# The seven-product stage of a three-part kernel: sums of weights on GpSimd, roundings a step behind, blocks of 256 and 320 tokens

## Chip, cores and metric

One NeuronCore of a Trainium2 chip. The metric is the device time of one execution in microseconds (us). Engines are named as the profile names them: PE (TensorE matmul), PEld (its weight loads), DVE (VectorE), ACT (ScalarE), POOL (GpSimd), SP (SyncE, which issues most of the transfers).

## What is computed

```python
def reference(q, k, v, w_in, w_out, w_gate, w1, w2):
    # 1. attention: pairs of queries are averaged, 2 batches x 8 heads, 1152 keys, 576 queries, 64 wide
    q_pool = q.reshape(2, 8, 576, 2, 64).mean(axis=3)
    a = softmax(q_pool @ k.transpose(0, 1, 3, 2) / 8) @ v
    x = a.transpose(0, 2, 1, 3).reshape(1152, 512)
    # 2. dense layer, 512 -> 2048 -> 512; w_in and w_out are float64
    h = x @ w_in
    x = (h * tanh(softplus(h))) @ w_out
    # 3. eight experts, 512 -> 1024 -> 512, weighted by a gate with 8 Sinkhorn rounds
    P = sinkhorn(exp(x @ w_gate))
    return sum(P[:, e:e+1] * (relu(x @ w1[e]) @ w2[e]) for e in range(8))
```

All of it is float32 arithmetic. The change lies in part 2.

## The kernel before

**Precision.** Every matmul operand is split into a rounded high part and a remainder (`split_hi`, L81 on ACT, `split_lo`, L88 on DVE or POOL). A product of two split operands is three matmuls: low times high, high times low, high times high.

**Part 2, plain stage.** The 2048 columns of `w_in` are done in four groups `i` of 512. Group 0 goes by plain products: twelve banks of 128 columns by 384 tokens, `mish_step(k)` for k = 0 to 11 (12 matmuls each, L259), with one more step, k = 12, behind them. What a step puts on ACT: the Mish of the bank before it and the rounding of its result (L285, L81), copies of finished output blocks (`out_sum`, L874 on ACT for the first half of the columns, L876 on DVE for the second), then what `run` finds due on the lists `queue[...]` ("pool", "act", "dve", "dma"), each with a due step. Output blocks (`out_bank`, L867, six matmuls of 384 tokens) use three PSUM banks "o". From the step in which they are ready, at most two follow the bank's products. Sixteen come in the steps 3, 4 and 7 to 12, the last eight behind step 12.

**Weights.** A quarter of a group's float64 weights (128 x 512) comes by one transfer from SP (L154) into a raw tile. ACT scales both halves (L167, L169), DVE shifts and joins bits (L182, L187), and POOL adds the low part (`join`, L193). `load_w` gives each of these a due step. The raw tiles are taken in turn: `raw_tile` uses one of `raw_tags` tags, three during attention and two from step 3 on, because the third tag (`raw2`) then holds `ut`, the temporaries of the seven-product stage. For `w_in` of groups 1 to 3 the result stays in float32 in `w32`. For `w_out` it is rounded on ACT and its remainder is taken on POOL (L88).

**Part 2, seven-product stage.** Groups 1 to 3 replace the 2 x 2 block product (two halves of the columns' pairs, two batches of tokens, two halves of the depth) by seven products of sums. The input sums T1 to T4 are made once, during the plain steps (`X_WORK`: `whole_x` L907 and `less` L910 on DVE over 128 x 1152 elements, `t_hi` on ACT, `t_lo` on POOL or DVE). The sums of the weights are made for each group and each half `f` by `operands(i, f)`, seven steps: four sums (L945, DVE, 128 x 256), seven roundings (L81, ACT) and seven remainders (L88, POOL), into the tiles `slots0` (f = 0) or `slots1` (f = 1). `unit(i, f, j)` runs the seven products (L979, six matmuls each) for half f and token block j of 288, with the output sums on DVE (L984, through `t1`, `u2`, `u3` in `ut`), a copy on ACT (L1000), and Mish and rounding (L992, L81) one or two events later.

**Order.** `phase` writes the order out by hand: a string of "m" (a product) and "q" (an output block, `out_block`, 12 matmuls of 288 tokens, L1035, added on DVE at L1038). After each of them `run_all` issues what is due on the lists, and after each "m" one step of `operands` follows. Group 1 starts with the last eight plain output blocks between its products; groups 2 and 3 run four phases of seven products and four output blocks:

```python
EVEN = "mmmqmqmqmmq"
phase(unit(i, 0, 0), qs[:4], prep, EVEN)   # prep: operands(i, 1)
phase(unit(i, 1, 0), qs[4:], [], EVEN)
phase(unit(i, 0, 1), qs[:4], [], EVEN)
phase(unit(i, 1, 1), qs[4:], [] if last else operands(i + 1, 0), EVEN)
```

In `unit` the product order is 1, 6, 5, 2, 7, 3, 4. Product 2 is added to the bank of product 1 after the copy t1 has been taken; product 4 is added to the bank of 6 and 7 after `u3` has been formed from it. The engines take their instructions in the order of the program. `operands(1, 0)` starts at step k = NB - 2 = 10 (`raise_slots`, `first_ops`); its tile takes the place of the plain stage's weights.

Part 3 (gate, experts) follows and isn't touched.

Of the kernel before, what the change touches and what calls it, by code (L numbers as in the profile page):

```python
# [8 lines left out]
F32 = mybir.dt.float32  # L9
# [14 lines left out]
def pool_attention_mish_sinkhorn_kernel(  # L24
# [301 lines left out]
    with ExitStack() as actx:  # L326
# [322 lines left out]
        def run_av(n):  # L649
# [13 lines left out]
        load_w(0, 1, [(t, t + 1, t + 2, 0, 0) for t in evenly(T0 + 4, 1.25)], 1)  # L663
        load_w(1, 1, [tuple(T0 + x for x in t) for t in (
            (9, 10, 11, 12, 12.4), (10, 11, 12, 12.5, 13), (12.3, 13, 13.7, 14.3, 14.9), (13.6, 14.3, 15, 15.6, 16.2))], 0.7)
# [173 lines left out]
    raw_tags = 2  # L839
    ut = wraw.tile([P, 2 * GF], F32, tag="raw2", name="ut")  # L840
# [37 lines left out]
    HB = SQ // 2  # L878

    def tokens(b, j):  # L880
        return slice(b * SQ + j * HB, b * SQ + (j + 1) * HB)

# [32 lines left out]
    def t_lo(n, k, eng):  # L915
# [4 lines left out]
        3: [lambda: whole_x(0, "12"), lambda: whole_x(1, "11")],  # L920
        4: [lambda: less(1, 0, 1), lambda: t_hi("T1", 1), lambda: whole_x(2, "22")],
        5: [lambda: t_lo("T1", 1, o_), lambda: less(0, 2, 0), lambda: t_hi("T3", 0)],
        6: [lambda: less(1, 2, 1), lambda: t_hi("T2", 1), lambda: t_lo("T3", 0, o_)],
        7: [lambda: whole_x(2, "21"), lambda: t_lo("T2", 1, v_)],
        8: [lambda: less(2, 2, 1)],
        11: [lambda: t_hi("T4", 2)],
        12: [lambda: t_lo("T4", 2, v_)],
# [12 lines left out]
    def operands(i, f):  # L940

        w = w32(i)
        a = lambda r, d: w[:, 2 * d:2 * d + 2, (2 * f + r) * P:(2 * f + r + 1) * P]
        def add(out, x, y, op, eng=nc.vector):
            eng.tensor_tensor(out=out, in0=x, in1=y, op=op)  # L945

        def split(n, x):
            hi, lo = slot(f, n)
            split_hi(nc.scalar, hi, x)
            split_lo(nc.gpsimd, lo, x, hi)  # L950

        return [
            lambda: (split(1, a(0, 0)), add(s1, a(1, 0), a(1, 1), ALU.add)),
            lambda: (split(5, s1), add(a(1, 0), a(0, 0), a(1, 0), ALU.subtract)),
            lambda: (add(a(0, 0), s1, a(0, 0), ALU.subtract), split(6, a(0, 0))),
            lambda: (split(2, a(0, 1)), split(7, a(1, 0))),
            lambda: add(a(0, 1), a(0, 1), a(0, 0), ALU.subtract),
            lambda: split(3, a(0, 1)),
            lambda: split(4, a(1, 1)),
        ]  # L960

    t1, u2, u3 = (ut[:, n * HB:(n + 1) * HB] for n in range(3))

    def unit(i, f, j):

        box = {}

        def mult(n):
            xn, bn = PRODUCT[n]
            if n in OPENS:  # L970
                box[bn] = ps_h.tile([P, 512], F32, tag="h", name=f"m{i}{f}{j}{bn}")[:, 0:HB]
            wh, wl = slot(f, n)
            x_h, x_l = XT[xn] if xn[0] == "T" else XB[xn]
            js = slice(j * HB, (j + 1) * HB)
            ops = []
            for d in range(2):
                ops += [(wl[:, d], x_h[:, d, js]), (wh[:, d], x_l[:, d, js]), (wh[:, d], x_h[:, d, js])]
            for m, (a_, b_) in enumerate(ops):
                nc.tensor.matmul(  # L979
                    box[bn], lhsT=a_, rhs=b_, start=n in OPENS and m == 0, stop=n in SHUTS and m == len(ops) - 1,  # L980
                    skip_group_check=True)
# [43 lines left out]
    def out_block(i, b, j, dc):  # L1025
        ps = ps_o.tile([P, 512], F32, tag="o", name=f"po{i}{b}{j}{dc}")
        tl = tokens(b, j)
        ds_ = slice(dc * P, (dc + 1) * P)
        ops = []
        whi, wlo = w2t[i]  # L1030
        for cc in range(NFC):
            gh, gl = hidden(cc, tl.start, tl.stop)
            ops += [(wlo[:, cc, ds_], gh), (whi[:, cc, ds_], gl), (whi[:, cc, ds_], gh)]
        for n, (a, b_) in enumerate(ops):
            nc.tensor.matmul(ps[:, 0:HB], lhsT=a, rhs=b_, start=(n == 0), stop=(n == len(ops) - 1))  # L1035
        step_pend()
        o = acc[:, dc, tl]
        pend.append((0, lambda: nc.vector.tensor_tensor(out=o, in0=ps[:, 0:HB], in1=o, op=ALU.add)))  # L1038

# [17 lines left out]
    first_ops = []  # L1057
    for k in range(EARLY, NB + 1):
# [3 lines left out]
        if k == NB - 2:  # L1062
            raise_slots()
        if k >= NB - 2:
            for _ in range((2, 3, 2)[k - NB + 2]):
                first_ops.pop(0)()
# [7 lines left out]
    xctx.close()  # L1074
    spacer(mctx, 64, "spb", side="right")
    wb = mctx.enter_context(tc.tile_pool(name="wb", bufs=1, side="right"))
    slots[1] = tuple(wb.tile([P, 7, 2, P], F32R, name=f"slots1{x}") for x in "hl")
# [8 lines left out]
    def phase(ms, qs, prep, order, dt=DTQ):  # L1086
        ms, qs = list(ms), list(qs)
        for c in order:
            if c == "m":
                event(ms.pop(0), DTM)  # L1090
                if prep:
                    prep.pop(0)()
            else:
                event(qs.pop(0), dt)
        assert not ms and not qs and not prep

    EVEN = "mmmqmqmqmmq"
    qs = [lambda x=x: old_block(*x[2:]) for x in todo]
    for i in range(1, NG1):
        last = i == NG1 - 1  # L1100
        prep = operands(i, 1)
        if i == 1:
            phase(unit(i, 0, 0), qs, prep, "qqmqmqmqmqmqmmq", DTO)
            phase(unit(i, 1, 0), [], [], "mmmmmmm")
# [510 lines left out]
```

## Time and profile before

| what | us |
|---|---|
| median of 3 runs | 1235.11 (1234.12 to 1237.66) |
| the profiled execution | 1235.38 |
| its span, first to last instruction | 1233.5 |
| busy: PE / DVE / ACT / POOL | 1193.0 / 925.2 / 610.5 / 675.7 |

The difference between the profiled time and the span (1.9 us) lies outside the instructions. Busy time is summed over an engine's instructions; matmuls overlap, so a busy PE need not be a PE at its peak. "Idle before" names what ended an engine's wait.

### The profile page before, as it was taken

What the parts mean: (1) busy time and instruction counts of PE and PEld (TensorE: products, weight loads), DVE (VectorE), ACT (ScalarE), POOL (GpSimd) and SP (SyncE); (2) the same over time, 40 slices, a digit from 0 to 9 for tenths busy, and PEclk for the clock granted to TensorE, in tenths of its full rate; (3) what the DMA queues carried; (4) which work ended last, traced back from release to release, by engine and by line L of the source; (5) the groups of instructions that cost most, each with busy time, mean ns of one, the idle gap of its engine ahead of it and who ended that gap; (6) DMA issues with size and microseconds to landing.
All of it is one profiled execution on the core that took longest, in us unless ns stands there. A gap on an engine that the chain in (4) does not pass through costs nothing.

```text
span 1233.5 us, 23493 instructions
## 1 busy us (share of the span) xinstructions
PE 1193.0 (97%) x8775; PEld 1172.9 (95%) x8775; DVE 925.2 (75%) x1708; ACT 610.5 (49%) x1431; POOL 675.7 (55%) x777
## 2 busy tenths in 40 slices
PE   8999999997798999999999999999999999999998
PEld 7999999996788989999999999999999999999998
DVE  7899999976586765578876766866877767866865
ACT  7899999864465544352333333333233333333331
POOL 7567777324546344355865555555556654555552
PEclk9999999998899999999999999999999999999999
DMA  5788887632122211001111111011111111110112
GB/s 195 262 287 279 279 280 261 228 119 86 44 94 85 84 38 60 18 10 52 44 52 52 52 53 52 26 46 42 52 52 44 52 52 52 52 45 30 45 46 78
DMA packets 53122, 116.66 MB, mean 95 GB/s; under 512 B 7976, under 2 KB 23536, under 8 KB 53008
## 3 DMA queue, kind: packets, MB, share of 16 engines
q1 hardware_dynamic: 50560, 106.31, 26.1%
q0 software_dynamic: 2448, 8.85, 2.5%
q8 instruction: 70, 1.15, 0.4%
q14 instruction: 44, 0.36, 0.1%
HBM read 66.86 MB, written 2.40 MB: 56 GB/s over the span
## 4 chain that ended last, share of the span: by engine, by line
PE 83%; DVE 7%; ACT 3%; issue 2%; DMA 2%; POOL 1%; DVEq 0%; POOLq 0%; ACTq 0%
PE po L1517 30%; PE c L1352 25%; PE psS L513 6%; PE psA L614 5%; PE po L1035 4%; PE psT L593 3%; PE ph L259 3%; DVE e L518 1%; DVE etl L599 1%; DMA er<-e 1%; DMA raw<-in_moe_w_in_dram 1%; PE psk L448 1%; PE po L867 1%; DVE xf L907 1%; ACT raw L167 1%
## 5 line engine op out<-in xcount | busy, mean ns | idle before, releaser
L1517 PE MATMUL po<-wdbl,hhall 128*128 128x256 f32 x1080 | 298.7, 277 | 0.0
L1517 PE MATMUL po<-wdbh,hlall 128*128 128x256 f32 x1080 | 298.3, 276 | 0.0
L1517 PE MATMUL po<-wdbh,hhall 128*128 128x256 f32 x1080 | 298.3, 276 | 0.0
L88 POOL TENSOR_TENSOR wslotsl<-s,wslotsh 128x256 fp32r<-128x256 f32 x180 | 132.6, 746 | 226.9 <-ACT wslotsh L81 225.5
L1526 DVE SCALAR_TENSOR_TENSOR oacc<-po,Pm,oacc 128x512 f32<-128x512 f32 (+1 forms) x217 | 161.2, 747 | 90.0 <-PE po L1517 85.1
L1517 PEld LDWEIGHTS po<-wdbl,hhall 128*128 128x128 f32 x1080 | 202.8, 188 | 0.0
L1517 PEld LDWEIGHTS po<-wdbh,hlall 128*128 128x128 f32 x1080 | 202.7, 188 | 0.0
L1517 PEld LDWEIGHTS po<-wdbh,hhall 128*128 128x128 f32 x1080 | 202.7, 188 | 0.0
L1369 ACT ACTIVATE t<-c 128x384 f32<-128x384 f32 x80 | 39.1, 489 | 234.2 <-PE c L1352 234.2
L1389 ACT ACTIVATE hhall<-c 128x384 fp32r<-128x384 f32 x180 | 88.5, 492 | 127.7 <-DVE c L1385 125.1
L88 POOL TENSOR_TENSOR wslotsl<-rawu,wslotsh 128x256 fp32r<-128x256 f32 x120 | 90.6, 769 | 49.5 <-ACT wslotsh L81 49.5
L599 DVE TENSOR_TENSOR etl<-psT,eth 128x384 fp32r<-128x384 f32 (+1 forms) x240 | 108.3, 510 | 7.5 <-ACT eth L596 6.9
L518 DVE TENSOR_SCALAR_CACHE_REDUCE e<-psS 128x1152 f32<-128x1152 f32 x72 | 97.7, 1356 | 16.3 <-PE psS L513 12.5
L1390 DVE SCALAR_TENSOR_TENSOR hlall<-c,hhall 128x384 fp32r<-128x384 f32 x180 | 98.8, 549 | 2.1
L596 ACT ACTIVATE eth<-psT 128x384 fp32r<-128x384 f32 (+1 forms) x240 | 92.1, 472 | 6.3 <-PE psT L593 5.9
L1352 PE MATMUL c<-x2h,wslotsl 128*128 128x384 f32 x280 | 94.3, 337 | 0.0
L1352 PE MATMUL c<-x2l,wslotsh 128*128 128x384 f32 x280 | 94.1, 336 | 0.0
L1352 PE MATMUL c<-x2h,wslotsh 128*128 128x384 f32 x280 | 94.1, 336 | 0.0
L532 ACT ACTIVATE e<-e,nm 128x1152 f32<-128x1152 f32 x70 | 89.2, 1274 | 2.8 <-DVE e L518 1.8
L81 ACT ACTIVATE wslotsh<-s 128x256 fp32r<-128x256 f32 x180 | 72.1, 411 | 25.3 <-DVE s L1318 23.9
L513 PE MATMUL psS<-kT,qT 128*128 128x384 f32 x384 | 81.3, 347 | 1.7 <-DVE e L518 1.2
L614 PE MATMUL psA<-etl,vst 128*128 128x256 f32 (+1 forms) x288 | 80.9, 303 | 0.8 <-DVE rs L541 0.4
(776 smaller groups left out, 3315.1 us busy)
## 6 DMA issues: line engine op xcount, KB each, us to landing
er<-e SPq DMA_DIRECT2D x70, 576.0 KB, 4.2
rawd<-in_moe_w_dram SPq DMA_DIRECT2D x60, 256.0 KB, 2.8
rawu<-in_moe_w_dram SPq DMA_DIRECT2D x30, 384.0 KB, 3.0
raw<-in_moe_w_in_dram SPq DMA_DIRECT2D x16, 512.0 KB, 6.1
raw<-in_moe_w_out_dram SPq DMA_DIRECT2D x16, 512.0 KB, 3.4
vraw<-in_v_dram POOLq DMA_DIRECT2D x15, 288.0 KB, 4.5
kraw<-in_k_dram POOLq DMA_DIRECT2D x13, 288.0 KB, 4.3
qT<-qT SPq DMA_DIRECT2D x28, 128.0 KB, 3.5
```

The costliest lines, as they stand in the source:

```text
L88: eng.tensor_tensor(out=lo, in0=src, in1=hi.bitcast(F32), op=ALU.subtract)
L513: nc.tensor.matmul(ps[:, kb, 0:TH], lhsT=a, rhs=kt[:, kb * TH:(kb + 1) * TH], start=(n == 0), stop=(n == len(ops) - 1))
L518: nc.vector.tensor_scalar(sc, ps[:, :, 0:TH], -1.0, None, op0=ALU.mult, op1=ALU.min, accum_out=nm)
L532: nc.scalar.activation(e, sc, AF.Exp, bias=nm, scale=-1.0, accum_out=rsS[p][:, t:t + 1])
L596: nc.scalar.activation(eh[:, cs, o:o + b - a], ps[:, 0:3, a:b], AF.Copy)
L599: nc.vector.tensor_tensor(out=el[:, cs, o:o + b - a], in0=ps[:, 0:3, a:b], in1=eh[:, cs, o:o + b - a].bitcast(F32), op=ALU.subtract)
L614: nc.tensor.matmul(box["ps"][:, 0:n], lhsT=vst[p, j][:, c].rearrange("p a d -> p (a d)"), rhs=(el, eh)[which][:, c, 0:n], start=(c == 0 an ...
L1352: nc.tensor.matmul(cb[c], lhsT=a_, rhs=b_, start=FIRST[n] and m == 0, stop=LAST[n] and m == len(ops) - 1, skip_group_check=True)
L1389: nc.scalar.activation(hi, b, AF.Relu)
L1390: los.append(lambda: nc.vector.scalar_tensor_tensor(out=lo, in0=b, scalar=0.0, in1=hi.bitcast(F32), op0=ALU.max, op1=ALU.subtract))
L1517: nc.tensor.matmul(ps[:, c0:c0 + 256], lhsT=a, rhs=b[:, cs.start + c0:cs.start + c0 + 256], start=(n == 0), stop=(n == len(ops) - 1))
L1526: nc.vector.scalar_tensor_tensor(out=oa, in0=ps[:, 0:w], scalar=gate, in1=oa, op0=ALU.mult, op1=ALU.add)
```

## The change

The sums of `w_in`'s blocks (four per `operands`) go from DVE to POOL, and `operands` has eight steps in place of seven, in which the remainder of an operand is issued one step after its rounding. In `phase` a step of it follows each event, not only each product. `operands(1, 0)` starts at step 12, not 10: four steps there and four behind the next four output blocks. Group 1's phases are reordered. The work on T1 to T4 is spread over more steps, each rounding a step behind its sum, and the remainders of T2 and T4 go from DVE to POOL. The third raw tag stays in use until step 7, and the due steps of group 1's weights shift a little. The token blocks are 256 and 320 in place of twice 288.

```diff
@@ -660,9 +660,9 @@
         load_w(1, 0, [(t, t + 1, t + 2, T0 + j, T0 + j + 1) for j, t in enumerate(QUIET[4:])], 2, "dve", busy=True)
         load_w(1, 0, [None, None] + [(t, t + 1, t + 2, t + 3, t + 4) for t in (T0 + 1, T0 + 3)], 1, "dve")
         G1, GT = T0 + NB, 28 * DTM + 16 * DTQ
-        load_w(0, 1, [(t, t + 1, t + 2, 0, 0) for t in evenly(T0 + 4, 1.25)], 1)
+        load_w(0, 1, [(T0 + t, T0 + t + 1, T0 + t + 2, 0, 0) for t in (4, 5, 6, 7)], 1)
         load_w(1, 1, [tuple(T0 + x for x in t) for t in (
-            (9, 10, 11, 12, 12.4), (10, 11, 12, 12.5, 13), (12.3, 13, 13.7, 14.3, 14.9), (13.6, 14.3, 15, 15.6, 16.2))], 0.7)
+            (10, 11, 12, 12.4, 12.8), (11, 12, 12.5, 13, 13.5), (13, 13.5, 14, 14.6, 15.2), (13.9, 14.5, 15.1, 15.7, 16.3))], 0.7)
         starts = [0, G1, G1 + 21 * DTM + 7 * DTM + 8 * DTQ + 8 * DTO]
         starts += [starts[2] + GT * x for x in (1, 2)]
         for i in range(2, NG1):
@@ -836,8 +836,6 @@
     tx_p = mctx.enter_context(tc.tile_pool(name="tx", bufs=1, side="right"))
     xctx = ExitStack()
     xf_p = xctx.enter_context(tc.tile_pool(name="xf", bufs=1, side="right"))
-    raw_tags = 2
-    ut = wraw.tile([P, 2 * GF], F32, tag="raw2", name="ut")
     accp = ctx.enter_context(tc.tile_pool(name="accp", bufs=1))
     spacer(ctx, 128, "sp9")
     hp_ = ctx.enter_context(tc.tile_pool(name="hp", bufs=1))
@@ -875,10 +873,11 @@
         else:
             nc.vector.tensor_tensor(out=o, in0=ps[:, 0:TH], in1=o, op=ALU.add)
 
-    HB = SQ // 2
+    JS = [slice(0, 2 * P), slice(2 * P, SQ)]
+    JN = [j.stop - j.start for j in JS]
 
     def tokens(b, j):
-        return slice(b * SQ + j * HB, b * SQ + (j + 1) * HB)
+        return slice(b * SQ + JS[j].start, b * SQ + JS[j].stop)
 
     def x2_split(b, j, dc):
         if "h" not in x2:
@@ -917,14 +916,14 @@
 
     v_, o_ = nc.vector, nc.gpsimd
     X_WORK = {
-        3: [lambda: whole_x(0, "12"), lambda: whole_x(1, "11")],
-        4: [lambda: less(1, 0, 1), lambda: t_hi("T1", 1), lambda: whole_x(2, "22")],
-        5: [lambda: t_lo("T1", 1, o_), lambda: less(0, 2, 0), lambda: t_hi("T3", 0)],
-        6: [lambda: less(1, 2, 1), lambda: t_hi("T2", 1), lambda: t_lo("T3", 0, o_)],
-        7: [lambda: whole_x(2, "21"), lambda: t_lo("T2", 1, v_)],
-        8: [lambda: less(2, 2, 1)],
-        11: [lambda: t_hi("T4", 2)],
-        12: [lambda: t_lo("T4", 2, v_)],
+        3: [lambda: whole_x(0, "12")],
+        4: [lambda: whole_x(1, "11"), lambda: less(1, 0, 1)],
+        5: [lambda: whole_x(2, "22"), lambda: t_hi("T1", 1)],
+        6: [lambda: less(0, 2, 0), lambda: t_lo("T1", 1, o_)],
+        7: [lambda: less(1, 2, 1), lambda: t_hi("T3", 0)],
+        8: [lambda: whole_x(2, "21"), lambda: t_hi("T2", 1), lambda: t_lo("T3", 0, o_)],
+        9: [lambda: less(2, 2, 1), lambda: t_lo("T2", 1, o_)],
+        12: [lambda: t_hi("T4", 2)],
     }
 
     UORD = [1, 6, 5, 2, 7, 3, 4]
@@ -941,37 +940,39 @@
 
         w = w32(i)
         a = lambda r, d: w[:, 2 * d:2 * d + 2, (2 * f + r) * P:(2 * f + r + 1) * P]
-        def add(out, x, y, op, eng=nc.vector):
-            eng.tensor_tensor(out=out, in0=x, in1=y, op=op)
-
-        def split(n, x):
-            hi, lo = slot(f, n)
-            split_hi(nc.scalar, hi, x)
-            split_lo(nc.gpsimd, lo, x, hi)
-
+        def add(out, x, y, op):
+            nc.gpsimd.tensor_tensor(out=out, in0=x, in1=y, op=op)
+
+        def h(n, x):
+            split_hi(nc.scalar, slot(f, n)[0], x)
+
+        def l(n, x):
+            split_lo(nc.gpsimd, slot(f, n)[1], x, slot(f, n)[0])
+
+        a11, a12, a21, a22 = a(0, 0), a(0, 1), a(1, 0), a(1, 1)
         return [
-            lambda: (split(1, a(0, 0)), add(s1, a(1, 0), a(1, 1), ALU.add)),
-            lambda: (split(5, s1), add(a(1, 0), a(0, 0), a(1, 0), ALU.subtract)),
-            lambda: (add(a(0, 0), s1, a(0, 0), ALU.subtract), split(6, a(0, 0))),
-            lambda: (split(2, a(0, 1)), split(7, a(1, 0))),
-            lambda: add(a(0, 1), a(0, 1), a(0, 0), ALU.subtract),
-            lambda: split(3, a(0, 1)),
-            lambda: split(4, a(1, 1)),
+            lambda: (add(s1, a21, a22, ALU.add), h(1, a11)),
+            lambda: (l(1, a11), add(a21, a11, a21, ALU.subtract), h(5, s1)),
+            lambda: (l(5, s1), add(a11, s1, a11, ALU.subtract), h(2, a12)),
+            lambda: (l(2, a12), h(6, a11)),
+            lambda: (l(6, a11), add(a12, a12, a11, ALU.subtract), h(7, a21)),
+            lambda: (l(7, a21), h(3, a12)),
+            lambda: (l(3, a12), h(4, a22)),
+            lambda: l(4, a22),
         ]
 
-    t1, u2, u3 = (ut[:, n * HB:(n + 1) * HB] for n in range(3))
-
     def unit(i, f, j):
 
         box = {}
+        t1, u2, u3 = (y[:, 0:JN[j]] for y in temps)
 
         def mult(n):
             xn, bn = PRODUCT[n]
             if n in OPENS:
-                box[bn] = ps_h.tile([P, 512], F32, tag="h", name=f"m{i}{f}{j}{bn}")[:, 0:HB]
+                box[bn] = ps_h.tile([P, 512], F32, tag="h", name=f"m{i}{f}{j}{bn}")[:, 0:JN[j]]
             wh, wl = slot(f, n)
             x_h, x_l = XT[xn] if xn[0] == "T" else XB[xn]
-            js = slice(j * HB, (j + 1) * HB)
+            js = JS[j]
             ops = []
             for d in range(2):
                 ops += [(wl[:, d], x_h[:, d, js]), (wh[:, d], x_l[:, d, js]), (wh[:, d], x_h[:, d, js])]
@@ -1032,10 +1033,10 @@
             gh, gl = hidden(cc, tl.start, tl.stop)
             ops += [(wlo[:, cc, ds_], gh), (whi[:, cc, ds_], gl), (whi[:, cc, ds_], gh)]
         for n, (a, b_) in enumerate(ops):
-            nc.tensor.matmul(ps[:, 0:HB], lhsT=a, rhs=b_, start=(n == 0), stop=(n == len(ops) - 1))
+            nc.tensor.matmul(ps[:, 0:JN[j]], lhsT=a, rhs=b_, start=(n == 0), stop=(n == len(ops) - 1))
         step_pend()
         o = acc[:, dc, tl]
-        pend.append((0, lambda: nc.vector.tensor_tensor(out=o, in0=ps[:, 0:HB], in1=o, op=ALU.add)))
+        pend.append((0, lambda: nc.vector.tensor_tensor(out=o, in0=ps[:, 0:JN[j]], in1=o, op=ALU.add)))
 
     def old_block(s, th, dc):
         o = out_bank(s, th, dc)
@@ -1055,14 +1056,18 @@
             todo += [(ready, SUBS[s], s, th, dc) for dc in range(NDC)]
     todo.sort(key=lambda x: x[0])
     first_ops = []
+    temps = []
     for k in range(EARLY, NB + 1):
         mish_step(k)
         for f in X_WORK.get(k, ()):
             f()
-        if k == NB - 2:
+        if k == NB - 5:
+            raw_tags = 2
+            ut = wraw.tile([P, 2 * GF], F32, tag="raw2", name="ut")
+            temps[:] = [ut[:, n * JN[1]:(n + 1) * JN[1]] for n in range(3)]
+        if k == NB:
             raise_slots()
-        if k >= NB - 2:
-            for _ in range((2, 3, 2)[k - NB + 2]):
+            for _ in range(4):
                 first_ops.pop(0)()
         room = NFC
         while todo and todo[0][0] <= k and room >= todo[0][1]:
@@ -1071,10 +1076,6 @@
             room -= n
     while outs:
         out_sum(*outs.pop(0))
-    xctx.close()
-    spacer(mctx, 64, "spb", side="right")
-    wb = mctx.enter_context(tc.tile_pool(name="wb", bufs=1, side="right"))
-    slots[1] = tuple(wb.tile([P, 7, 2, P], F32R, name=f"slots1{x}") for x in "hl")
     now = T0 + NB
 
     def event(f, dt):
@@ -1088,20 +1089,26 @@
         for c in order:
             if c == "m":
                 event(ms.pop(0), DTM)
-                if prep:
-                    prep.pop(0)()
             else:
                 event(qs.pop(0), dt)
+            if prep:
+                prep.pop(0)()
         assert not ms and not qs and not prep
 
     EVEN = "mmmqmqmqmmq"
     qs = [lambda x=x: old_block(*x[2:]) for x in todo]
+    t_lo("T4", 2, o_)
+    phase([], qs[:4], first_ops, "qqqq", DTO)
+    xctx.close()
+    spacer(mctx, 64, "spb", side="right")
+    wb = mctx.enter_context(tc.tile_pool(name="wb", bufs=1, side="right"))
+    slots[1] = tuple(wb.tile([P, 7, 2, P], F32R, name=f"slots1{x}") for x in "hl")
     for i in range(1, NG1):
         last = i == NG1 - 1
         prep = operands(i, 1)
         if i == 1:
-            phase(unit(i, 0, 0), qs, prep, "qqmqmqmqmqmqmmq", DTO)
-            phase(unit(i, 1, 0), [], [], "mmmmmmm")
+            phase(unit(i, 0, 0), qs[4:6], prep, "mmmqmqmmm", DTO)
+            phase(unit(i, 1, 0), qs[6:], [], "mmqmmqmmm", DTO)
         else:
             phase(unit(i, 0, 0), qs[:4], prep, EVEN)
             phase(unit(i, 1, 0), qs[4:], [], EVEN)
```

## Rows read from the trace of the kernel before

**Rows 1.** The page, part 1: busy time, share and count by engine.
```profile
PE 1193.0 (97%) x8775; PEld 1172.9 (95%) x8775; DVE 925.2 (75%) x1708; ACT 610.5 (49%) x1431; POOL 675.7 (55%) x777
```
**Rows 2.** Two stretches: start:end, length, busy us by engine, granted clock, DMA.
```profile
281.60:349.60 68.00, 49.19 (x255) 46.15 (x254) 42.04 (x69) 35.51 (x76) 32.95 (x28) 0.90 0.22 70
384.00:451.00 67.00, 59.40 (x433) 57.63 (x434) 46.46 (x99) 34.89 (x84) 34.60 (x34) 1.00 0.26 79
```
**Rows 3.** PE's waits, 281 to 350: total us, times, longest.
```profile
PE po L867 <- DVE acc L876: 7.3, 3, 3.4
PE po L867 <- ACT hhall L81: 4.0, 1, 4.0
PE po L867 <- ACT acc L874: 4.0, 2, 2.6
PE m110B L979 <- ACT ut L1000: 2.0, 1, 2.0
```
**Rows 4.** PE's waits, 350 to 452.
```profile
PE m210B L979 <- DVE ut L984: 2.1, 2, 1.4
PE m200B L979 <- DVE ut L984: 2.1, 1, 2.1
PE m300B L979 <- DVE ut L984: 1.9, 1, 1.9
PE m210B L979 <- ACT ut L1000: 1.4, 1, 1.4
```
**Rows 5.** Timeline of ACT: start, us, instruction, [idle before it <- releaser].
```profile
284.23 1.16 ACT L81 ACTIVATE T3h<-xf 128x1152 fp32r<-128x1152 f32 x1 [5.00 <-DVE xf L910]
...
314.52 0.42 ACT L81 ACTIVATE slots0h<-w 128x256 fp32r<-128x256 f32 x1 [4.35 <-PE ph L259]
...
380.60 0.42 ACT L81 ACTIVATE slots1h<-w 128x256 fp32r<-128x256 f32 x1 [2.58 <-DVE w L945]
```
**Rows 6.** ACT's waits for transfers, 280 to 350.
```profile
ACT raw L167 <- DMA raw<-in_moe_w_in_dram: 8.6, 3, 4.5
```
**Rows 7.** Timeline of POOL, 274 to 286.
```profile
275.22 2.32 POOL L193 TENSOR_TENSOR wt<-wt,raw 128x512 int32<-128x512 int32 x1 [4.15 <-PE po L867]
277.69 3.62 POOL L88 TENSOR_TENSOR T1l<-xf,T1h 128x1152 fp32r<-128x1152 f32 x1 [0.15 <-ACT T1h L81]
...
285.47 2.62 POOL L88 TENSOR_TENSOR T3l<-xf,T3h 128x1152 fp32r<-128x1152 f32 x1
```
**Rows 8.** Timeline of DVE, 269 to 284.
```profile
269.83 3.73 DVE L907 TENSOR_TENSOR xf<-xh,xl 128x1152 f32<-128x1152 f32 x2
...
276.27 2.48 DVE L907 TENSOR_TENSOR xf<-xh,xl 128x1152 f32<-128x1152 f32 x1
...
279.15 2.71 DVE L88 TENSOR_TENSOR wdl<-wt,wdh 128x512 fp32r<-128x512 f32 x1
281.79 0.41 DVE L182 TENSOR_SCALAR w<-raw 128x512 uint32<-128x512 uint32 x1
...
282.84 1.35 DVE L910 TENSOR_TENSOR xf<-xf,xf 128x1152 f32<-128x1152 f32 x1
```
**Rows 9.** Timeline of POOL, 342 to 345: a join, the last remainder of slots1.
```profile
342.86 1.29 POOL L193 TENSOR_TENSOR wt<-wt,raw 128x512 int32<-128x512 int32 x1
344.10 0.73 POOL L88 TENSOR_TENSOR slots1l<-w,slots1h 128x256 fp32r<-128x256 f32 x1
```
**Rows 10.** Timeline of DVE: one sum of weights.
```profile
363.03 0.41 DVE L945 TENSOR_TENSOR s<-w 128x256 f32<-128x256 f32 x1
```
**Rows 11.** Timeline of PE: first and last of twelve matmuls, 384 tokens, then 288.
```profile
264.07 0.33 PE L259 MATMUL ph<-xh,wul 128*128 128x384 f32 x1
...
265.97 0.34 PE L259 MATMUL ph<-xh,wuh 128*128 128x384 f32 x1
...
351.95 0.30 PE L1035 MATMUL po<-hhall,wdl 128*128 128x288 f32 x1
...
353.40 0.29 PE L1035 MATMUL po<-hhlast,wdh 128*128 128x288 f32 x1
```

## The prediction, made before the change was run

> **What bounds the kernel now.** I read the page first: PE has work for 97% of the span [rows 1], so a change that leaves PE's work alone can only gain what PE waits. Windows then show where that is: from 281.6 to 349.6 PE is busy for 49.2 of 68.0 us at a granted clock of 0.90, and from 384 to 451 for 59.4 of 67.0 us [rows 2]. These are the end of the plain stage with group 1, and the first three quarters of group 2 with the start of group 3.
>
> In the first stretch PE has 20 plain output blocks (120 matmuls of 384 columns), four plain banks (48 of them) and 14 products (84 of 288). Eleven starts apart, the pitch is 0.173 us at 384 columns and 0.132 at 288 [rows 11]. That makes 20.8 + 8.3 + 11.1 = 40.2 us of work in 68.0: 27.8 us are lost. The list of waits names 17.3 us of it, 15.3 of them output blocks of the plain stage that wait for ACT or DVE [rows 3]; the rest is smaller waits and the lower clock behind the long ones.
>
> ACT's timeline tells why ACT is late. The rounding T3h waits 5.00 us for the sum that DVE makes in the same step; the first rounding of slots0 waits 4.35 us for a plain bank's matmuls, whose weights lie where slots0 comes to lie [rows 5]; and 8.6 us go into three waits for transfers of `w_in` [rows 6], which start only when one of two raw tiles is free. A Mish and the copies of output blocks stand behind each of these.
>
> DVE is late for another reason. POOL's join starts at 275.22 and ends at 277.54; DVE's sum that starts at 276.27 shows 2.48 us, to 278.75. POOL's T1l starts at 277.69 and shows 3.62, against 2.62 for T3l; and DVE's remainder of 279.15 shows 2.71 and ends 0.5 us after T1l [rows 7, 8]. Each stands until the other is done, and takes its own time then: such a DVE instruction and one of POOL exclude each other. I call this the shared path. DVE instructions whose first input is in PSUM don't show it.
>
> In the second stretch 7.5 us are waits for `u2`, `u3` or `t1` [rows 4]. Behind one stands ACT, which waits 2.58 us for a sum of weights [rows 5] that DVE made late because POOL had the path.
>
> **The change, part by part.**
> *Third raw tile until step 7, due steps.* Quarters 1 and 2 of group 1 no longer wait for the join of the one before. Quarter 3 takes the tile of quarter 0 and still does. I keep some 3.5 us of the 8.6.
> *Roundings a step behind sums.* The 5.00 us of ACT go, and with them PE's longest wait of 4.0 us [rows 3]. What is late next is DVE, which has the same sums to make.
> *slots0 from step 12.* The 4.35 us go, as the last plain bank is done by then. In exchange POOL gets its whole batch of operands only then; four plain output blocks (24 x 0.173 = 4.2 us) cover half of it.
> *T2l and T4l to POOL.* 2.62 in place of some 1.35 us each (a sum of DVE of that size [rows 8]), both on the shared path.
> *Sums of weights to POOL.* A sum on DVE takes 0.41 us [rows 10]. POOL's sum of 128 x 256 isn't in the trace; the nearest row is its remainder of the same size, 0.73 [rows 9]. Below, it could be no dearer than DVE's 0.41; above, it is hardly dearer than a join of twice the elements, 1.29. I take 0.73, the same kind of instruction at the same size. DVE saves 1.6 us per batch, the shared path gets 1.3 more. One wait is new: a rounding on ACT now waits for POOL's queue, and behind it stand Mish, t1 and the copies of output blocks.
> The Trainium skill, GPSIMD Engine Reference, section Engine selection, speaks against this part: it gives elementwise work with two inputs to VectorE and calls GpSimd about twice as slow. The rows say 1.8 times; at twice, the sum below grows by 0.7 us for eight sums.
> *Blocks of 256 and 320.* The pitch per column is the same at 288 and at 384 (0.46 and 0.45 ns [rows 11]), so the two blocks cost PE what two of 288 cost. But 84 matmuls x 32 columns x 0.46 ns = 1.2 us move out of the first stretch and are paid later; a program that reaches group 1's second block earlier has gained 1.2 us less than it seems. Copies and Mish split the same way: nothing.
> *SP's order* keeps its transfers; they are only issued earlier or later. Nothing is queued behind them but other raw tiles.
>
> **The sum for the first stretch.** What remains is the shared path. From 269.8, where DVE starts the first input sum [rows 8], to the last remainder of slots1 it must carry: on POOL nine joins (11.6 us), four remainders T1l to T4l at 2.62 (10.5), 14 remainders and 8 sums at 0.73 (16.1), two of `w_out` as dear as a join (2.6); on DVE eight input sums at 1.35 (10.8), nine shifts with their sign at 1.05 (281.79 to 282.84 [rows 8]; 9.5), two remainders (1.2). Together 62.3 us: not before 332.1. The same count of before is 57.1 us, and it ended at 344.8 [rows 9]: the path was taken for 76% of 75.0 us. I take 94% for after, three quarters of the way to a full path, since the waits for transfers and for the bank shrink and hand-overs stay: 66.3 us, so 336.1. PE was through 4.8 us after that last remainder (349.6), and I keep this distance, because ACT will stand in front of a sum of POOL at product 4 of group 1's first unit instead. That gives 340.9, less 349.6: 8.7 us earlier, of which 1.2 are the moved columns: a gain of 7.5 us. Bounds: a full path and PE 0.9 us behind it give 349.6 - 333.0 - 1.2 = 15.4; a path taken for 76% as before gives 269.8 + 82.0 + 4.8 = 356.6, a loss of 8.2.
>
> **The second stretch.** Two batches of operands follow each other there in 24 us, each with 1.3 us more on the shared path. For it speaks that DVE doesn't stand in front of the path for sums of weights any more, eight times in these two phases; against it, that POOL runs late and ACT waits for it. Of 7.5 us I give back 3, with bounds of 7.5 and of -3 (the same waits and twice 1.3 more).
>
> Sum: 1235.4 (the profiled execution; its span of 1233.5 and 1.9 around it; the median of the runs is 0.3 lower) - 7.5 - 3 = 1224.9, so **1225 us**. In place of a range from the extremes alone, 1217 to 1231 is the likeliest case's own.
>
> **Rivals.**
> *A: the shared path doesn't bind* (chance 0.20). For it: DVE and POOL exclude each other only where both want it at the same moment, and in the second stretch POOL is busy for 34.6 of 67.0 us [rows 2]. Then PE bounds the stretch: 40.2 - 1.2 us and some 7 us of short waits, 46 of 68.0, less the 1.2: a gain of 21; with 3 to 5 in the second stretch 1209 to 1212.
> *B: the waits only change their names* (0.12). ACT waits for POOL's sums as long as it waited for DVE's and the transfers; PE stands in front of group 1 for POOL's batch. The path is taken for some 83%: 75 us, to 344.8, gains 0 to 2: 1233 to 1236.
> *C: slower* (0.08): POOL falls behind. In each of the four late batches (two of group 2, two of group 3) POOL gets 11 instructions of 0.73 us, 8.0 us, in eight events of 8.7 us (five products of 6 and three output blocks of 12 matmuls at 0.132), beside two or three joins and remainders of 1.29 each and DVE's shifts. If POOL starts a batch later than some 3 us, the rounding of the third operand sum holds ACT until the bank that product 5 of the next unit needs is late: 2 to 3 us a batch, 8 to 12 in all, against a gain of no more than 4 in the first stretch: 1240 to 1243. It decides from the point at which POOL's lag exceeds the 3 us between product 4 and the next product 5 (an output block and two products, 24 x 0.132). This is also what the skill's rule on engine selection would make of it.
> The forecast has 0.60.
>
> **Chances.** Runs of before differ by 0.3% between lowest and highest, so under 0.3% (3.7 us, 1231.4 to 1238.8) counts as no change. The forecast and A are faster (0.80), B is the same (0.12), C slower (0.08). The range leaves out C and a part of both A and B: 1210 to 1234.
>
> **What the profile after would show.** Right: no wait of T3h for `xf` near 284 and no wait of slots0h for a plain bank; one wait for a `w_in` transfer in place of three; L945's successor on POOL at about 0.73 us; POOL without a pause from step 12 to the last remainder of slots1, that one between 334 and 338; PE's longest wait in group 1's first unit, for a DVE result that stands behind ACT and this behind POOL; the first product of group 1's second block near 341; PE's pitch per column unchanged. Wrong: pauses of POOL there (then the path isn't the bound, A), a Mish that waits as long as before (B), or waits of PE between 384 and 451 in new places that sum to more than 8 us (C). The prediction fails if DVE and POOL overlap more than the rows let me see, or if a sum on POOL costs nearer a join.

## The result and the profile after

The changed kernel takes 1220.3 us (1219.2 to 1221.1, 4 runs) beside 1234.6 for the kernel before: a ratio of 0.988, 95% interval 0.986 to 0.990. It is 14 us faster, where 10 were forecast. The profiled execution has a span of 1218.8 us, against 1233.5.

The page, busy time by engine, to be read against [rows 1]. PE is busy 4.7 us less, POOL 26.1 more:
```profile
PE 1188.3 (97%) x8775; PEld 1169.5 (96%) x8775; DVE 919.0 (75%) x1682; ACT 611.2 (50%) x1431; POOL 701.8 (58%) x803
```
The windows of [rows 2], on the kernel after:
```profile
281.60:349.60 68.00, 56.07 (x341) 54.34 (x340) 53.13 (x75) 38.48 (x84) 51.03 (x41) 0.92 0.24 78
384.00:451.00 67.00, 66.14 (x497) 65.50 (x496) 43.23 (x95) 34.33 (x83) 34.54 (x35) 1.00 0.19 64
```
In the same 68 us PE now does 341 instructions, not 255, and POOL works for 51.0 us, not 33.0. In the second window PE has no gap worth the name: 66.1 of 67.0 us.

PE's waits from 268 to 345, then from 345 to 452, for [rows 3, 4]:
```profile
PE m100B L980 <- DVE ut L985: 6.8, 1, 6.8
PE po L865 <- ACT acc L872: 2.6, 1, 2.6
PE m100B L980 <- ACT ut L1001: 1.6, 1, 1.6
PE m100B L980 <- POOL slots0l L88: 0.8, 1, 0.8
PE po L865 <- DVE hlall L88: 0.7, 1, 0.7
...
PE m200B L980 <- DVE ut L985: 2.0, 1, 2.0
PE m300B L980 <- DVE ut L985: 0.5, 1, 0.5
```
The output blocks of the plain stage (`po`) keep 3.3 us of the 16.0 us that they waited in this window before (15.3 in that of [rows 3], which leaves out one wait of 0.7). One long wait is new, 6.8 us at product 4 of group 1's first unit. The second list sums to 3.7 us.

ACT's waits from 268 to 345, then two of its instructions and the last two stretches of POOL's run, for [rows 5, 6, 9]:
```profile
ACT slots0h L81 <- POOL w L944: 6.1, 2, 3.1
ACT raw L167 <- DMA raw<-in_moe_w_in_dram: 5.4, 3, 3.8
...
ACT slots1h L81 <- POOL w L944: 3.3, 1, 3.3
```
```profile
288.44 1.15 ACT L81 ACTIVATE T3h<-xf 128x1152 fp32r<-128x1152 f32 x1
...
324.56 0.42 ACT L81 ACTIVATE slots1h<-w 128x256 fp32r<-128x256 f32 x1 [3.26 <-POOL w L944]
```
```profile
305.67 0.74 POOL L944 TENSOR_TENSOR s<-w 128x256 f32<-128x256 f32 x1
...
325.86 0.72 POOL L944 TENSOR_TENSOR w<-w 128x256 f32<-128x256 f32 x1
327.67 1.28 POOL L193 TENSOR_TENSOR wt<-wt,raw 128x512 int32<-128x512 int32 x1 [1.09 <-DVE wt L187]
328.91 2.31 POOL L88 TENSOR_TENSOR slots1l<-w,slots1h 128x256 fp32r<-128x256 f32 x3
```
T3h waits no more, the waits for a plain bank are gone from in front of the operands, and ACT stands in front of POOL's sums instead. A sum on POOL takes 0.74 us. From 304.4 to 331.2 POOL is at work for 25.1 of 26.8 us, and the last remainder of slots1 ends at 331.2, against 344.8.

The stage of attention ends at slightly different times from run to run, so I count from the first output block of step 3 (269.0 us before, 270.3 after). All numbers of this table are read off the timelines, in us from that instruction:

| kernel | last remainder of slots1 | first product of group 1's second block | first matmul of the gate | end of span |
|---|---|---|---|---|
| before | 75.8 | 80.5 | 220.1 | 964.5 |
| after | 60.9 | 68.7 | 203.4 | 948.5 |
| third tile alone | 69.7 | 74.9 | 215.5 | 960.4 |
| third tile, due steps | 72.3 | 77.4 | 219.3 | 964.1 |
| after, two raw tiles | 73.1 | 80.7 | 216.5 | 961.6 |
| after, T4's remainder three times | 66.3 | 74.8 | 209.4 | 954.5 |
| after, sums on DVE | 57.9 | 67.8 | 205.6 | 950.7 |
| after, old input sums | 62.9 | 71.0 | 205.7 | 951.1 |
| after, operands from step 10 | 61.4 | 69.1 | 203.9 | 949.3 |
| after, blocks of 288 | 61.0 | 69.0 | 202.8 | 947.9 |
| after, `w_out` quarter later | 58.5 | 70.2 | 204.8 | 949.7 |
| after, operands(1, 1) later | 63.0 | 67.3 | 201.9 | 947.3 |
| after, both later | 65.0 | 70.9 | 206.3 | 951.6 |
| after, operands(1, 1) later, blocks of 288 | 62.7 | 67.1 | 200.4 | 945.4 |

So 11.8 us come up to group 1's second block, 4.9 more up to the gate; 0.7 are lost behind it, and the profiled run began 1.3 later: 14.7 in the span. Each row is one profiled execution; where kernels differ by a microsecond or two, the intervals of their runs, given below, often overlap.

### The profile page after: what moved, and what is told of

It is laid out like the page before. It is cut to its first block, busy times and chain, and to the rows that moved or that the text cites. A ratio compares the mean times of both kernels' runs of the same rounds, so it can differ in the third digit from the quotient of the medians.

```text
span 1218.8 us, 23492 instructions
## 1 busy us (share of the span) xinstructions
PE 1188.3 (97%) x8775; PEld 1169.5 (96%) x8775; DVE 919.0 (75%) x1682; ACT 611.2 (50%) x1431; POOL 701.8 (58%) x803
## 4 chain that ended last, share of the span: by engine, by line
PE 67%; POOL 1%; ACT 0%; DVE 0%; issue 0%; POOLq 0%
PE po L1524 30%; PE c L1359 26%; PE po L1036 4%; PE ph L259 2%; PE m311B L980 1%; PE m211B L980 1%; PE m201B L980 1%; PE m301B L980 1%; PE pg L1153 0%; PE m310B L980 0%; POOL w L944 0%; PE m210B L980 0%; PE po-1_8_0_0_7149 L1524 0%; PE po-1_0_0_0_6894 L1524 0%; PE po-1_7_0_0_7113 L1524 0%; PE po-1_6_0_0_7081 L1524 0%
## 5 line engine op out<-in xcount | busy, mean ns | idle before, releaser
L1524 PEld LDWEIGHTS po<-wdbh,hlall 128*128 128x128 f32 x1080 | 202.8, 188 | 0.0
L1524 PEld LDWEIGHTS po<-wdbh,hhall 128*128 128x128 f32 x1080 | 202.8, 188 | 0.0
```

The costliest lines, as they stand in the source:

```text
L1524: nc.tensor.matmul(ps[:, c0:c0 + 256], lhsT=a, rhs=b[:, cs.start + c0:cs.start + c0 + 256], start=(n == 0), stop=(n == len(ops) - 1))
```

## The experiments

My theory was the prediction's: with the transfers and ACT's stalls out of the way, the shared path of DVE and POOL sets the end of the first stretch. Rivals: the third raw tile does it all; or ACT's order does, the path having slack. Ratios are to the kernel before, with 95% intervals.

**What does the 6.8 us wait hang on?** ACT's late Mish (behind the rounding that waits 3.26 us for POOL), or DVE's shift ahead of the unit's sums? DVE's timeline after shows both:
```profile
319.99 6.88 DVE L182 TENSOR_SCALAR wt<-raw 128x512 uint32<-128x512 uint32 x1
326.90 0.69 DVE L187 SCALAR_TENSOR_TENSOR wt<-raw,wt 128x512 uint32<-128x512 uint32 x1
```
The shift, 0.41 us in [rows 8], shows 6.88. Nine POOL instructions stand back to back from 319.79 to 326.58, and it ends 0.3 us after POOL's first pause. ACT's Mish starts at 326.28: both chains end together. Three kernels pull them apart.

*late_shift: the shift of one `w_out` quarter a step later, that of the next 0.4 later.*
```diff
-(13, 13.5, 14, 14.6, 15.2), (13.9, 14.5, 15.1, 15.7, 16.3)
+(13, 14.5, 14.7, 15.1, 15.5), (13.9, 14.9, 15.3, 15.7, 16.3)
```


> The changed kernel, with one edit: the shift of w_out's third quarter of group 1 is due at 14.5 in place of 13.5 (the steps behind it follow), so that DVE has it behind u3 of group 1's first unit. In the changed kernel this shift shows 6.88 us and PE then waits 6.8 us for product 4. Path theory (DVE stands behind POOL's unbroken run of operands, and this alone makes u3 late): the wait falls to under 2 us, the time to 1214 to 1216. ACT theory (the rounding of the third operand sum holds ACT, and the Mish and the remainder ahead of u3 stand behind it): the wait falls by no more than 1 us, the time is 1219 to 1220.

Measured 1221.8, 0.988 (0.987 to 0.990). The wait fell only to 6.0, as the theory of ACT's order had it, and one of 2.3 us came at the second unit's product 4; the time is above both expectations. With the shift out of the way, DVE's remainder ahead of the sums stands for ACT instead (DVE's timeline):
```profile
326.61 0.42 DVE L88 TENSOR_TENSOR hlall<-m100B,hhall 128x256 fp32r<-128x256 f32 x1 [6.56 <-ACT hhall L81]
```

*late_prep: operands(1, 1) begin three events later.*
```diff
-            if prep:
+            if prep and n >= skip:    # n counts the events
...
-            phase(unit(i, 0, 0), qs[4:6], prep, "mmmqmqmmm", DTO)
-            phase(unit(i, 1, 0), qs[6:], [], "mmqmmqmmm", DTO)
+            phase(unit(i, 0, 0), qs[4:6], prep, "mmmqmqmmm", DTO, 3, 2)   # skip 3, leave 2
+            phase(unit(i, 1, 0), qs[6:], prep, "mmqmmqmmm", DTO)
```


> The changed kernel, with the eight steps of operands(1, 1) begun three events later in group 1's first phase, the last two in the second phase, so that on ACT the first Mish stands ahead of the rounding that waits for POOL's sum. ACT theory: PE's wait for product 4 falls from 6.8 to under 2 us, the time to 1214 to 1216. Path theory: DVE's shift still stands behind POOL, the wait stays over 5 us and the time at 1218 to 1221.

Measured 1218.5, 0.986 (0.984 to 0.987), the wait between the two expectations. PE's longest wait, in its list of waits, and the shift in DVE's timeline:
```profile
PE m100B L980 <- DVE ut L985: 3.4, 1, 3.4
```
```profile
320.61 3.48 DVE L182 TENSOR_SCALAR wt<-raw 128x512 uint32<-128x512 uint32 x1
```
With ACT's stall out of the first unit the shift still shows 3.48 us, up to 0.3 us behind POOL's first pause. The edit moves POOL's row too: it pauses after four instructions beside the shift, at 323.80, not after nine. So ACT's chain alone makes a wait of 6.0 us (late_shift); what DVE's chain alone would make of the long row isn't shown, only that it makes 3.4 us with the short one.

*late_both.*

> Both edits: the late shift and the late operands. If each of the two alone is enough to make u3 late, only this one takes the wait of 6.8 us away. Then PE waits in group 1's second unit for the operands themselves, whose last remainder comes at 331 in the changed kernel: 4 to 6 us are gained, 1214 to 1216. If one of the single edits gains that already, this one gains no more than 1 us on it.

Measured 1223.7, 0.990 (0.988 to 0.992), not the 1214 to 1216 expected. The first wait is down to 1.8, the shift to 2.04, as both causes together should give. But the join behind the later shift frees its raw tile later than in late_prep: SP issues the next transfer at 328.07, there at 326.20, or 3.5 us later counted from step 3. ACT waits for the next transfer in front of a rounding, and PE pays at the second unit (ACT's timeline, PE's waits):
```profile
332.03 0.65 ACT L167 ACTIVATE raw<-raw 128x512 f32<-128x512 f32 x1 [3.60 <-DMA raw<-in_moe_w_in_dram]
```
```profile
PE m110B L980 <- DVE ut L985: 6.5, 1, 6.5
```
That loss is a side effect of the edit; late_shift pays it too (ACT waits 3.49 us for the same transfer).

**Which part carries the gain?** Parts of the change undone one at a time.

*sums_on_dve: the sums of weights on DVE again.*
```diff
-            nc.gpsimd.tensor_tensor(out=out, in0=x, in1=y, op=op)
+            nc.vector.tensor_tensor(out=out, in0=x, in1=y, op=op)
```


> The changed kernel, with the sums of weights back on DVE and all else as changed. By the count of the shared path alone each sum takes 0.41 in place of 0.73 us, eight of them ahead of the last remainder of slots1: 1 to 3 us faster, 1217 to 1219. By queues: DVE stands in front of the path for each of them, and u2, u3 and the copies stand behind: 3 to 8 us slower than the changed kernel, 1223 to 1228.

Measured 1220.8, 0.987 (0.986 to 0.989): no different from after, and between the two expectations. The table says why. POOL's run ends 3.0 us earlier, but PE is only 0.9 earlier at the second block, and by group 3 the gain is lost: there DVE's sum waits for a remainder on POOL, and PE for DVE (DVE's timeline, PE's waits):
```profile
422.77 0.93 DVE L944 TENSOR_TENSOR w<-w 128x256 f32<-128x256 f32 x1 [2.74 <-POOL slots1l L88]
```
```profile
PE m300B L980 <- DVE ut L985: 2.9, 1, 2.9
```

*blocks_288.*
```diff
-    JS = [slice(0, 2 * P), slice(2 * P, SQ)]
+    JS = [slice(0, SQ // 2), slice(SQ // 2, SQ)]
```


> The changed kernel with two token blocks of 288 again in place of 256 and 320. By the pitch per column nothing changes: within 2 us of the changed kernel, 1218 to 1222. The rival, that the block sizes carry a part of the gain (less work for PE and DVE while group 1's operands are made): 1.2 us come back in the first stretch and nothing is returned later, or PE's waits for operands change by more than 2 us.

Measured 1218.8, 0.987 (0.985 to 0.988). The blocks carry nothing that shows.

*x_old: X_WORK as before (T2l and T4l on DVE again).* The diff is the one shown of `X_WORK`, backwards, with `t_lo("T4", 2, o_)` left out behind step 12.

> The changed kernel with the input sums T1 to T4 in the steps and on the engines of before (each rounding in the step of its sum, T2l and T4l on DVE). The wait of the rounding T3h for its sum returns and with it PE's wait of some 4 us near 284; against it 2.5 us less on the shared path. Forecast: 1 to 4 us slower, 1221 to 1224. If the path alone counts: 1 to 3 us faster, 1217 to 1219.

Measured 1222.9, 0.990 (0.988 to 0.992): 2.6 us later at the end of the profiled execution. The 4.0 us wait of [rows 3] is back:
```profile
PE po L865 <- ACT hhall L81: 4.0, 1, 4.0
```

*slots_early: operands(1, 0) from step 10 again.*
```diff
-        if k == NB:
+        if k == NB - 2:
             raise_slots()
-            for _ in range(4):
+        if k >= NB - 2:
+            for _ in range((2, 3, 3)[k - NB + 2]):
                 first_ops.pop(0)()
```


> The changed kernel with group 1's first operands begun at step 10 again (two, three and three of the eight steps at steps 10, 11 and 12). Their first rounding must wait for the last plain bank, as before: ACT stands 3 to 5 us, the Mish of bank 10 and the output blocks behind it are late. Forecast: 3 to 6 us slower, 1223 to 1226. If POOL's run of operands is the bound, its earlier start is worth as much: 1218 to 1221.

Measured 1220.8, 0.989 (0.987 to 0.990), not clear of after; 0.8 us later at the end of the profiled execution. PE's wait at product 4 fell from 6.8 to 5.6 us, and three waits of output blocks for DVE came, 3.5 together: what POOL's earlier start gives, the plain stage pays.

*raw_two: two raw tiles from step 3 on, the rest of the change kept.*
```diff
+    raw_tags = 2
+    ut = wraw.tile([P, 2 * GF], F32, tag="raw2", name="ut")
     for k in range(EARLY, NB + 1):
...
-        if k == NB - 5:
-            raw_tags = 2
-            ut = wraw.tile([P, 2 * GF], F32, tag="raw2", name="ut")
```


> The changed kernel with two raw tiles from step 3 on, as before, and the due steps as changed. If transfers set ACT's lateness in the plain stage, 3 to 6 us of ACT's waits return and 2 to 5 us of the gain go: 1222 to 1225. If the shared path sets it, the plain stage ends at the same time: 1219 to 1221.

Measured 1233.1 (10 runs), 0.998 (0.997 to 0.999). Both expectations missed: 13 of the 16 us go with the tile. ACT's timeline has the cause, POOL's the effect:
```profile
287.59 0.66 ACT L167 ACTIVATE raw<-raw 128x512 f32<-128x512 f32 x1 [10.10 <-DMA raw<-in_moe_w_in_dram]
288.69 1.15 ACT L81 ACTIVATE T1h<-xf 128x1152 fp32r<-128x1152 f32 x1
```
```profile
289.96 2.65 POOL L88 TENSOR_TENSOR T1l<-xf,T1h 128x1152 fp32r<-128x1152 f32 x1 [6.53 <-ACT T1h L81]
...
317.99 0.74 POOL L944 TENSOR_TENSOR s<-w 128x256 f32<-128x256 f32 x1
```
The rounding T1h stands behind the transfer, T1l behind T1h, and POOL's run of operands begins at 317.99, not 305.67. It is the same run, with the same pause of 1.09 us, moved by 12.2 us, and everything behind it moves with it.

**Is the tile all, then?** The other way round: the kernel before with the tile, and with tile and due steps.
```diff
-    raw_tags = 2
-    ut = wraw.tile([P, 2 * GF], F32, tag="raw2", name="ut")
     accp = ctx.enter_context(tc.tile_pool(name="accp", bufs=1))
...
+        if k == NB - 5:
+            raw_tags = 2
+            ut = wraw.tile([P, 2 * GF], F32, tag="raw2", name="ut")
+            temps[:] = [ut[:, n * HB:(n + 1) * HB] for n in range(3)]
```


> The kernel before with one thing of the change: the third raw tile stays in use until step 7. Due steps, input sums, operands, sums on DVE and blocks of 288 as before. Tile theory (formed from the run with two raw tiles, in which nearly the whole gain went): the transfers' wait for a free raw tile is what held ACT in the plain stage, so this alone gives 8 to 13 us, 1222 to 1227, and the first product of group 1's second block moves forward by as much. Prediction's theory (the path of DVE and POOL sets the end of the stretch, the tile takes only some 3.5 us out of ACT's waits): 1230 to 1234, with the 5.0 us wait of T3h and the 4.35 us wait for the plain bank still there. A third possibility: the old due steps don't start the transfers any earlier, then no change.

Measured 1232.3 (10 runs), 0.997 (0.996 to 0.998). PE's waits, then ACT's timeline:
```profile
PE po L865 <- DVE acc L874: 7.4, 3, 3.4
PE po L865 <- ACT hhall L81: 4.0, 1, 4.0
```
```profile
286.18 1.16 ACT L81 ACTIVATE T3h<-xf 128x1152 fp32r<-128x1152 f32 x1 [5.00 <-DVE xf L908]
...
309.20 0.67 ACT L167 ACTIVATE raw<-raw 128x512 f32<-128x512 f32 x1 [6.65 <-DMA raw<-in_moe_w_out_dram]
```
ACT's waits for `w_in` fell from 8.6 to 2.2 us, but those for `w_out` rose from 3.6 to 8.1. The longest stands in front of the first rounding of slots0, which then no longer waits for the plain bank, as it had been expected to. T3h's 5.00 us stayed, and so did PE's waits of 7.3 and of 4.0 us for `hhall` [rows 3]; those for copies on ACT went. The time is the one of the prediction's theory.

> The kernel before with the third raw tile until step 7 and the changed due steps of group 1's weights, nothing else. Tile theory: 1220 to 1225, all or nearly all of the change's gain, so that the sums on POOL, the spread of the input sums and the later start of the operands carry little between them. If the parts work only together (the freed time is taken by the sums that DVE makes late and by the bank's wait of slots0): 1230 to 1234, and the run with two tiles lost its 13 us because everything else of the change stands on the third tile.

Measured 1233.9 (10 runs), 0.998 (0.997 to 0.999). In the profiled executions the new due steps in the old order lose nearly all that the tile gave (0.4 us are left); the runs alone, with overlapping intervals, don't show it. The first rounding of slots0 waits longer for the plain bank than the 4.35 us of [rows 5]:
```profile
306.91 0.42 ACT L81 ACTIVATE slots0h<-w 128x256 fp32r<-128x256 f32 x1 [6.21 <-PE ph L259]
```
So, from step 3 to the end, the tile alone gives 4.1 us, the rest without it 2.9, both together 16.0; the ratios of the runs say 3.3, 2.3 and 14.9.

**Has POOL's run slack?** T4's remainder taken three times, so two idle repetitions on POOL.
```diff
-    t_lo("T4", 2, o_)
+    for _ in range(3):
+        t_lo("T4", 2, o_)
```


> The changed kernel with the remainder of T4 taken three times in place of once: two more POOL instructions of 2.7 us behind step 12, in the middle of the stretch in which POOL has hardly a pause (304 to 331). Prediction's theory (POOL and what excludes it set the end of the stretch): the last remainder of slots1 comes 5.4 us later and the first product of group 1's second block as much, less the pause of 1.1 us: 4 to 5.4 us slower, 1224 to 1226. Rival (the stretch ends by ACT's and DVE's order, and POOL's operands have slack once the raw tiles come in time): under 2 us slower, 1220 to 1222.5.

Measured 1227.7, 0.993 (0.992 to 0.995): by the ratios 6.7 us more than after, a little above the forecast of the prediction's theory. POOL's timeline, then PE's waits:
```profile
312.76 8.05 POOL L88 TENSOR_TENSOR xl<-xf,xh 128x1152 fp32r<-128x1152 f32 x3
...
335.88 2.31 POOL L88 TENSOR_TENSOR slots1l<-w,slots1h 128x256 fp32r<-128x256 f32 x3
```
```profile
PE m100B L980 <- POOL slots0l L88: 6.1, 1, 6.1
```
5.4 us of work move the last remainder by 5.4, the second block and the end by 6.0. PE meets it at once, in the first products, since POOL gives it slots0 just in time: up to slots0 POOL's run has no slack.

For the rest of the run this isn't shown. The table has three kernels in which the last remainder of slots1 and the second block don't move together: with late_shift the run ends 2.4 us earlier and the block comes 1.5 later; with late_prep the run ends 2.1 us later and the block comes 1.4 earlier; with the sums on DVE the run ends 3.0 us earlier and the block 0.9. Behind slots0 the waits at product 4 of the two units decide, not the last remainder.

**A version ahead of the change?** late_prep with blocks of 288.

> The changed kernel with operands(1, 1) begun three events later (its last two steps in the next phase) and blocks of 288 again: the two edits that came out a little ahead of the changed kernel, each within its uncertainty. If both are real they add up: 1.2 and 0.6 us in the time from the first output block of step 3, so 1217.5 to 1219. If they are noise, 1219.5 to 1221.

Measured 1218.8 (1214.4 to 1219.5, 4 runs), 0.986 (0.983 to 0.988). In the profile it is 3.1 us shorter from step 3, and the wait at product 4 is down to 1.9. That is more than the two edits should add up to, and the shift tells why: it comes in behind one POOL instruction, without a pause of POOL (DVE's timeline, then POOL's).
```profile
320.77 1.31 DVE L182 TENSOR_SCALAR wt<-raw 128x512 uint32<-128x512 uint32 x1
```
```profile
320.49 1.30 POOL L88 TENSOR_TENSOR wdl<-wt,wdh 128x512 fp32r<-128x512 f32 x1
321.76 0.91 POOL L944 TENSOR_TENSOR s<-w 128x256 f32<-128x256 f32 x1
```
The interval overlaps that of the change (0.986 to 0.990), so it is not shown to be faster.

## Why the prediction was right, point by point

**The path.** I took the busy intervals of POOL and of DVE's instructions without PSUM input, from the first input sum to the last remainder of slots1, and counted the time that either covers. Before: 56.6 of 75.0 us (75%; the prediction counted 57.1). After: 57.9 of 60.1 (96%; it said 62.3 at 94%). With two raw tiles 58.4 of 72.3, with T4's remainder three times 63.1 of 65.5 (96%), with the sums on DVE 54.1 of 57.1 (95%). In the last, POOL alone is busy for 42.8 of the 57.1 us, so it is the pair that fills the stretch and not POOL's queue; after the change POOL alone is busy for 47.4 of the 60.1. What the path must carry hardly changes; the change fills its holes. The share was right, the sum 4.4 us too large. Which of its terms was, the records don't tell, since a duration there includes the time in which an instruction stood. The Trainium skill, SBUF — State Buffer, section "Who interferes with whom", has a mechanism: DVE and GpSimd share a pair of ports; a DVE instruction in a mode with two ports contends with GpSimd for it, and whoever issues first holds it for the whole instruction; one with two inputs in SBUF contends with GpSimd's reads. The trace agrees with it for single instructions [rows 7, 8]; the shift of 6.88 us goes further, as it stood through nine of them, and which of the two cases the shift is no run here shows. A full path is not by itself what ends the stretch, though: the repetition shows no slack up to slots0, and behind it the wait at product 4 comes on top.

**The first stretch** is the term that was mis-sized: the second block was forecast 8.7 us earlier (7.5 without the moved columns), and it came 11.8 earlier (11.5 without them). The prediction ended POOL's run 66.3 us after the first input sum and PE's part 4.8 behind it; measured were 60.1 and 7.8, the latter for the wait at product 4, which it had placed there (DVE behind ACT behind POOL), without the shift that shares it. The 1.2 us set off for the narrower first block was 0.3 in the run with blocks of 288, as PE had waits there to absorb it.

**The third tile.** The prediction kept 3.5 of the 8.6 us that ACT waits for `w_in`; in the kernel after 5.4 us are left, 3.2 less. Alone the tile is worth 3.3 to 4.1 us of time. But as an item of a sum it was treated wrongly. The parts are in series: transfers, ACT's roundings of T1 and T3, POOL's T remainders, POOL's run of operands. As long as one of them is late, removing another gives little.

**Roundings a step behind, slots0 from step 12:** the waits named went. Undoing the first (with T2l and T4l) costs 2.6 us in the profile, the second 0.8; the intervals of both overlap that of after.

**Sums on POOL:** 0.73 was taken, 0.74 measured. The prediction charged them 1.3 us a batch on the path; with them POOL's run is 3.0 us longer over both batches of group 1 (the covered time 3.8), but the gate is reached 2.2 us sooner in the profiled execution. The rule of the Trainium skill's GPSIMD Engine Reference, section Engine selection, holds for the instruction (0.74 beside 0.41 us [rows 10]) and not for the kernel: on POOL the sum and the remainder that reads its operand stand in one queue, with no engine waiting for another.

**The second stretch** gave 4.9 us to the gate, 5.2 with the moved columns, against 3 forecast and a bound of 7.5. Most of it goes with the sums on POOL: from the second block to the gate the ten kernels that have them there take 133.3 to 135.8 us, the changed kernel with the sums on DVE 137.8, and the three with the old order of operands 139.6 to 141.9, in one profiled execution each. PE's waits there from 350 on, 8.1 us in all (7.5 in the lines of [rows 4]), became 3.7; none of 2 to 3 us came new, so rival C is out. **A** is out by the time, by POOL's run with no pause above 1.1 us and by the repetition that costs 6.0 us; **B** by the gain, though it is what the change gives with two raw tiles. Of the signs, POOL's run, T3h, the bank and product 4 came as said; the transfers of `w_in` still make three waits, but only one above 1.5 us; the last remainder came at 331.2, ahead of 334 to 338, and the second block's first product at 339.0, for 341.

**Open:** why the shift waits for the end of POOL's row of instructions at 319.99, while one at 307.19 takes 0.90 us in the midst of such a row, and the same one in prep_288 1.31; and how much of the 13 us with two raw tiles belongs to the new due steps.

## What to carry to other kernels

When two engines exclude each other, count the time that either is busy and compare it with the stretch: 75% said here that there was room and something else started the work late; at 96% 5.4 us of added work cost 6.0. It doesn't follow that less work helps: 3.8 us less on the path (the sums on DVE) brought the next block 0.9 us forward and the end not at all. Ask what waits next before the path is shortened. Waits in series don't add: test a part both by taking it out of the finished change and by putting it alone into the old kernel (here 13.1 and 4.1 us for the same tile). And an instruction that is slower on another engine may still cost nothing there, if it spares a hand-over between two queues.

## What was unexpected of the hardware

A DVE shift of 0.41 us stood for 6.88 us behind nine POOL instructions that followed each other without a pause; it was let in only when POOL paused, and not between two of them. In four other kernels (two raw tiles, T4's remainder three times, old input sums, blocks of 288) the same shift stood for 6.82 to 6.97 us, each time up to POOL's first pause; in prep_288 it came in behind the first instruction. In the fourteen traces this shift takes more than 0.6 us 131 times, and every time it ends 0.28 or 0.29 us after the end of a POOL instruction.
